# Batch 0's q and k by two hardware queues, its v ahead of w_in, and v's shifts by SyncE's queue

## The chip, the cores and the metric

The kernel runs on one core of one Trainium2 chip. The metric is the device time of one execution in microseconds. The engines are PE (matrix), PEld (its weight loads), DVE (vector), ACT (scalar), POOL (GpSimd) and SP (SyncE). Each runs its own instructions in the order in which the program was written, and waits on semaphores. SP and ACT issue DMAs on a hardware queue each, POOL issues DMAs on a software queue; a DMA that casts fp32 to bf16 on the way is issued by POOL here.

## The reference

```python
scores = q @ k.T / sqrt(64)                    # 8 batches, 8 heads, 576 positions, 64 wide
mask   = (0 <= i - j) & (i - j < 64)           # causal, a window of 64
attn   = softmax(where(mask, scores, -1e9))
x      = (attn @ v) -> 4608 tokens x 512       # heads side by side
h      = x @ w_in                              # 512 x 2048
out    = (h * sigmoid(h)) @ w_out              # 2048 x 512, fp32
```

All inputs are fp32 in DRAM.

## The kernel before, in words

**Attention.** Queries are cut into blocks of 64; a "visit" does 3 or 4 blocks of all 8 heads. Visits 0, 1, 2 are blocks 0 to 2, 3 to 5, 6 to 8: all of batch 0. A visit is a chain over four engines: scores on PE (`scores`, L298; for batch 0 the mask is first added by a matmul of `ident` with `bias`, L290), exp on ACT (L305), for later batches a mask product on DVE (L314), values on PE (`values`, L331), then on DVE the reciprocal (L337), the normalisation (L342) and a transpose into `bridge` (L350), which the feed-forward part reads. The scores of all visits use the PSUM banks 0 to 3, so a visit's scores wait for the exp of the visit before.

**Feed-forward.** Tokens go in tiles of 512 (j = 0 to 8; the first layer of j = 0 also does columns up to 576). The first layer is L360 (`first_layer`, `w_in_sb` in 16 column groups ft of 128, four matmuls each), silu on ACT is L366, the second layer is L369 for j = 0 and 1 and the products of L400 from j = 2 on. Exp and silu need different tables in ACT; a change of table is an ACT_TABLE_LOAD.

**Loads.** q and k of batches 0 and 1 come in three thirds c of 192 positions, for two groups Q of four heads: `load_rows` (L234) on POOL's queue, one DMA for each of q, k and Q. They land in `natq`, `natk`; DVE transposes them into `qt`, `kt` (L281). In batch 0's third 0, the heads of Q = 1 come as fp32 by `load_first` (L247), one DMA of 32 partitions for each head: q by SP's queue, k by ACT's; `cast_first` (L251) casts them. v comes in four groups g of 128 positions (`load_v`, L240) into `vo`, and 64 positions at the end straight into `ve` (L243). `ve` is v shifted by 64 positions, needed by even blocks; for batches 0 and 1 it is filled from `vo` by copies of half the partitions (`copy_v`, L262, DVE or ACT, up and down for each g), for later batches by two DMAs on SP's queue (L256, L258). w_in comes in 8 DMAs (L265), w_out in 8 (L269), by POOL's queue.

**What sets the order.** The kernel writes its operations down with costs, dependencies and ranks (`Plan.add`), and `Plan.run` simulates the engines and emits each engine's instructions in the order that its own model gives; operations of one class stay in the order in which they were added. So the order on POOL's queue is the order of the `p.add("dma", ...)` calls, and that on PE, ACT and DVE follows from the model's costs. When no attention work is ready, PE runs fillers on a tile of zeros (`warm`, L661) until the first layer has begun; their number and place are fixed by the plan. POOL's DMAs and the hardware DMAs each take eight semaphores in turn, so the ninth waits for the landing of the first.

In the kernel before, POOL issues: q and k of third 0 (Q = 0), v groups 0 and 1, w_in's first quarter (two DMAs), third 1, the constants `ident` and `window` (L191 to L199), v group 2, w_in's second quarter, third 2, v group 3 and the end of v, w_in's rest, w_out 0 to 3, then batch 1 with w_out 4 to 7 between its pieces. PE does the first layer of ft 0 to 3 for visit 0's columns (192 wide) between visits 0 and 1, the same for visit 1's columns before visit 2's values, and then ft 4 to 15 in widths of 384 and 192.

Of the kernel before, what the change touches and what calls it, by code (L numbers as in the profile page):

```python
# [15 lines left out]
class Plan:  # L16
# [10 lines left out]
        self.count = 0  # L27
        self.now = 0.0

    def add(self, cls, us, fn, deps=(), lat=0.1, gate=None, dma=None, pool=None, table=None, first=None):  # L30
        op = dict(us=us, first=self.rank[cls] if first is None else first, fn=fn, deps=[d for d in deps if d is not None],
                  lat=lat, gate=gate, dma=dma, pool=pool, table=table, seen=None, n=self.count, until=[], bank=None, cls=cls)
        self.count += 1
        self.queues.setdefault(cls, []).append(op)
        return op
# [13 lines left out]
    def run(self):  # L49
# [9 lines left out]
        while left:  # L59
            if not events:  # L60
                raise RuntimeError([(c, head[c], len(q), q[head[c]]["n"]) for c, q in self.queues.items() if head[c] < len(q)])
            now = self.now = heapq.heappop(events)
            while events and events[0] == now:
                heapq.heappop(events)
            moved = True
            while moved:
                moved = False
                for e in engines:
                    if free[e] > now:
                        continue  # L70
# [24 lines left out]
                    if op["table"] and op["table"] != table:  # L95
                        table, us = op["table"], us + 1.28
                    if e == "PE":
                        m = {"s": "rows", "v": "cols"}.get(c[0] if c in ("s", "v", "s0", "v0") else "", "full")
                        if m != mode:
                            mode, us = m, us + 0.1  # L100
                    end = free[e] = now + us
                    if op["dma"] is None:
                        op["seen"] = end + op["lat"]
                    else:
                        soft = e == "POOL"
                        begin = max(pipe[soft], end + (1.3 if soft else 0.8))
                        pipe[soft] = begin + op["dma"] * (1.0 if soft or pipe[True] < begin else 2.0)
                        op["seen"] = pipe[soft] + (2.2 if soft else 1.8) + (2.0 if soft and now > 45 else 0.0)
# [17 lines left out]
def kernel(ctx, tc, q, k, v, w_in, w_out, out):  # L126
    nc = tc.nc
# [45 lines left out]
    raw = gsum.rearrange("p s f t -> p (s f t)").bitcast(FP32)[:, 0:2 * NM * D].rearrange("p (k x) -> p k x", k=2)  # L173
# [5 lines left out]
    p = Plan(  # L179
        {"at": lambda: [(0, 1, 2, 3)], "two": lambda: [(4, 5), (6, 7)],  # L180
         "mp": lambda: [(i,) for i in (range(8) if att_end and p.done(att_end) else range(4, 8))]},
        rank=dict(one=-9, late=6, dma=-1, ldk=-9, ldq=-9, st=-2, vs=-3, silu=-3, out=-2, keep=-2.1, ssum=-1.2, tsum=1.2,
                  s=1, v=0, moe=99, warm=200, exp=1, mask=1, inverse=0, norm=0.1, cross=0.2, turn=2, cast=-4,
                  prime=-8, s0=-5.5, v0=-5.6, exp0=-4.6, inverse0=-4.3, norm0=-4.2, cross0=-4.25, turn0=-4, copy=1.5, copy0=-4.05),
    )
    copies = {"ACT": nc.scalar.copy, "DVE": nc.vector.tensor_copy, "POOL": nc.gpsimd.tensor_copy}

# [225 lines left out]

    rows_in, v_in, turned, turn_last = {}, {}, {}, {}
    s_last, v_last = {}, {}
    win, wout = {}, {}

# [33 lines left out]
    def add_first():  # L453
        for kk in range(2):
            rows_in[(0, kk, 0, 0)] = p.add("dma", {"POOL": 0.67}, lambda _, kk=kk: load_rows(0, kk, 0, 0), dma=0.55)
            ld = [p.add("ldk" if kk else "ldq", {"ACT" if kk else "SP": 0.45}, lambda _, kk=kk, h=h: load_first(kk, h), dma=0.14)
                  for h in range(4, 8)]
            rows_in[(0, kk, 0, 1)] = p.add("cast", {"ACT": 0.5, "DVE": 0.36}, lambda e, kk=kk: cast_first(e, kk), ld)

    def need_rows(vi):  # L460
        need = set()
# [5 lines left out]
    def need_v(vi):  # L467
        ops = []
        for x in range(vi["nb"]):
            b, t = divmod(vi["n0"] + x, NB)  # L470
            ops += v_in[(b, t // 2)] + (v_in[(b, t // 2 - 1)] if t % 2 == 0 and t else [])
        return list({o["n"]: o for o in ops}.values())


# [12 lines left out]
    def gate_scores(vi):  # L487
        def may():
# [3 lines left out]
            op, kind, rest, tile = x  # L492
            if tile < vi["tile"] - 2:
                return False
            if kind == 1:
                return not p.done(op["deps"]) and rest > 0
            return rest > 10
# [181 lines left out]
    c_ident = p.add("dma", {"POOL": 0.6}, const_ident)  # L679
    c_window = p.add("dma", {"POOL": 0.6}, const_window)  # L680
    c_bias = p.add("one", {"DVE": 0.5}, const_bias, [c_window])
    c_mask = p.add("late", {"DVE": 0.6}, const_mask, [c_window])
# [13 lines left out]
    add_w_out(5)  # L696
    add_rows(1, 1)
    add_v(1, 2)
    add_w_out(6)
    add_w_out(7)  # L700
    add_rows(1, 2)
    add_v(1, 3)
    add_v(1, 4)
    for c in range(NC):
        add_turns(0, c)
# [6 lines left out]
        add_turns(1, c)  # L712
    add_copies(1)
    gts = {0: {ft: (2 * ft, []) for ft in range(NFT)}, 1: {ft: (2 * ft + 1, []) for ft in range(NFT)}}
    for ft in range(0, 4):
        add_part(0, [ft], gts[0], 0, 192, 1)
    for ft in range(0, 4):
        add_part(0, [ft], gts[0], 192, 384, 1)
    for ft in range(4, 16):
        add_part(0, [ft], gts[0], 0, 384, 1)  # L720
    for ft in range(16):
        add_part(0, [ft], gts[0], 384, 576, 1)
        gts[1][ft][1].extend(gts[0][ft][1][-1:])
    add_second(0, gts[0], True)
    add_visit(visits[3])
# [71 lines left out]
```

## Time and profile before

| | |
|---|---|
| median of 3 runs | 334.33 us (299.22, 334.33, 415.25) |
| the profiled execution | 299.01 us |
| its span in the profile | 297.2 us |
| granted PE clock | 1.00 in every stretch |
| PE busy, with fillers | 281.5 us, 95% |
| DVE, ACT, POOL busy | 173.7, 166.0, 119.6 us |
| software DMA queue | 82656 packets, 18.20 MB |
| hardware queues of SP and ACT | 12.88 MB and 0.20 MB |

The profile is one execution. Its page gives the busy share by engine and slice, the chain of work that ended last and the costliest groups; beside it stand the timeline of each engine (start, duration, engine, line, tiles, count, and in brackets the idle time before and what ended it), sums over stretches, and the landings of DMAs. A DMA's landing is the last of the updates of its semaphore.

### The profile page before, as it was taken

How to read it: one execution, taken by the hardware profiler on the slowest of the kernel's cores; microseconds unless marked ns; L12 is line 12 of the kernel's file. 1: busy time of each engine (PE TensorE's matmuls, PEld its weight loads, DVE VectorE, ACT ScalarE, POOL GpSimd, SP SyncE). 2: the span in 40 equal slices, each digit the busy share in tenths (PEclk: the TensorE clock that was granted, in tenths of full speed). 3: DMA queues.
4: the chain of work that ended last, by engine and by line, in shares of the span. 5: the costliest groups of instructions: out<-in, count | busy, mean ns of one | idle time of the engine just before them, and what ended most of it. 6: DMA issues, size and time to landing. Idle time of an engine off the chain costs nothing.

```text
span 297.2 us, 9200 instructions
## 1 busy us (share of the span) xinstructions
PE 281.5 (95%) x4000; PEld 184.3 (62%) x4008; DVE 173.7 (58%) x327; ACT 166.0 (56%) x258; POOL 119.6 (40%) x183
## 2 busy tenths in 40 slices
PE   8973999999999999899999999999999999999993
PEld 4553584488444488447864686478647854884682
DVE  2464247561497498976986597469446944333412
ACT  1567792498618771767266835673477346316620
POOL 8787587887879779869600000000000000000000
PEclk9999999999999999999999999999999999999999
DMA  8999999999999999999996003000300030012003
GB/s 101 159 149 197 179 155 172 114 211 192 147 179 199 153 163 124 245 165 129 84 153 182 2 2 118 25 2 4 142 2 2 2 146 0 0 40 104 2 18 124
DMA packets 89512, 31.86 MB, mean 107 GB/s; under 512 B 76672, under 2 KB 84352, under 8 KB 89472
## 3 DMA queue, kind: packets, MB, share of 16 engines
q0 software_dynamic: 82656, 18.20, 66.4%
q1 hardware_dynamic: 6624, 12.88, 13.8%
q8 instruction: 31, 0.51, 0.7%
q10 hardware_dynamic: 192, 0.20, 0.2%
q14 instruction: 9, 0.07, 0.1%
HBM read 36.70 MB, written 9.44 MB: 155 GB/s over the span
## 4 chain that ended last, share of the span: by engine, by line
PE 76%; DMA 14%; POOL 5%; DVE 2%; issue 1%; DVEq 0%; POOLq 0%
PE ps L360 37%; PE ps L400 29%; DMA natq<-in_q_dram 8%; PE ps L369 5%; PE ps L331 3%; PE ps L298 3%; DMA w_in_sb<-in_moe_w_in_dram 3%; DMA ve<-in_v_dram 2%; POOL w_out_sb L269 1%; POOL vo L240 1%; DMA natk<-in_k_dram 1%; POOL natq L229 1%; POOL w_in_sb L265 1%; POOL natk L234 1%; POOL natq L234 1%
## 5 line engine op out<-in xcount | busy, mean ns | idle before, releaser
L360 PE MATMUL ps<-bridge,w_in_sb 128*128 128x512 bf16 (+3 forms) x720 | 127.4, 336 | 4.6 <-DVE bridge L350 2.8
L366 ACT ACTIVATE g<-ps 128x512 bf16<-128x512 f32 (+3 forms) x180 | 90.5, 512 | 43.3 <-PE ps L360 42.3
L360 PEld LDWEIGHTS <-w_in_sb 128*128 128x128 bf16 x720 | 67.8, 98 | 61.0 <-DVE bridge L350 3.0
L392 DVE TENSOR_TENSOR gsum<-g 128x512 bf16<-128x512 bf16 x56 | 23.5, 419 | 48.8 <-ACT g L366 48.8
L400 PEld LDWEIGHTS <-gsum 128*128 128x128 bf16 x448 | 43.2, 98 | 5.3
L400 PE MATMUL ps<-g,gsum 128*128 128x256 bf16 x336 | 42.6, 273 | 0.0
L305 ACT ACTIVATE e<-ps 128x2048 bf16<-128x2048 f32 (+1 forms) x19 | 34.0, 1787 | 13.8 <-PE ps L298 13.6
L400 PEld LDWEIGHTS <-g 128*128 128x128 bf16 x336 | 31.8, 98 | 4.6
L229 POOL DMA_DIRECT2D natk<-in_k_dram x48 | 28.9, 613 | 9.3 <-DMA vo<-in_v_dram 5.3
L240 POOL DMA_DIRECT2D vo<-in_v_dram x32 | 28.8, 915 | 6.5 <-PE ps L331 2.7
L229 POOL DMA_DIRECT2D natq<-in_q_dram x48 | 29.0, 620 | 3.3 <-issue 1.3
L403 ACT COPY part<-ps 128x256 f32<-128x256 f32 x27 | 10.1, 373 | 35.2 <-PE ps L400 35.2
L369 PE MATMUL ps<-w_out_sb,g 128*128 128x512 bf16 x120 | 27.6, 379 | 1.1 <-issue 1.0
L400 PE MATMUL ps<-w_out_sb,g 128*128 128x256 bf16 x224 | 26.8, 273 | 0.0
L314 DVE TENSOR_TENSOR e<-e,mask 128x2048 bf16<-128x2048 bf16 (+1 forms) x16 | 19.3, 1206 | 10.6 <-ACT e L305 10.3
L350 DVE STREAM_TRANSPOSE bridge<-ob 128x1024 bf16<-128x1024 bf16 (+1 forms) x19 | 22.3, 1173 | 0.2
L342 DVE TENSOR_TENSOR ob<-ps,rc 128x1024 bf16<-128x1024 f32 (+1 forms) x19 | 22.0, 1158 | 0.4
L412 DVE TENSOR_TENSOR ot<-ps,part 128x256 f32<-128x256 f32 (+1 forms) x35 | 16.2, 470 | 9.9 <-PE ps L400 5.4
L369 PEld LDWEIGHTS <-g 128*128 128x128 bf16 x128 | 11.8, 98 | 13.6
L281 DVE STREAM_TRANSPOSE qt<-natq 128x192 uint32<-128x192 uint32 x12 | 6.2, 519 | 19.4 <-DMA natq<-in_q_dram 19.4
L298 PEld LDWEIGHTS <-kt 32*128 32x128 bf16 x1152 | 10.7, 92 | 8.6 <-issue 5.9
L400 PE MATMUL ps<-g 128*128 128x256 bf16 x112 | 15.9, 273 | 0.0
(53 smaller groups left out, 226.3 us busy)
## 6 DMA issues: line engine op xcount, KB each, us to landing
out_dram<-ot SPq DMA_DIRECT2D x34, 256.0 KB, 3.0
vo<-in_v_dram POOLq DMA_DIRECT2D x32, 128.0 KB, 6.0
natq<-in_q_dram POOLq DMA_DIRECT2D x48, 72.0 KB, 5.1
natk<-in_k_dram POOLq DMA_DIRECT2D x48, 72.0 KB, 3.9
ve<-vo SPq DMA_DIRECT2D x12, 264.0 KB, 5.2
w_in_sb<-in_moe_w_in_dram POOLq DMA_DIRECT2D x8, 256.0 KB, 7.3
w_out_sb<-in_moe_w_out_dram POOLq DMA_DIRECT2D x8, 256.0 KB, 7.7
natq<-in_q_dram POOLq DMA_DIRECT2D x11, 96.0 KB, 7.7
```

Of the source, the lines that this page charges most:

```text
L229: nc.gpsimd.dma_start(out=nats[kk][b % NK][r, h // 4].rearrange("p c x -> p (c x)").rearrange("p (t x) -> p t x", x=2 * D), in_=(q, k)[kk] ...
L240: nc.gpsimd.dma_start(out=vos[b % NV][:, g, :, 0:D], in_=v[b, :, 128 * g:128 * g + 128].rearrange("h p d -> p h d"))
L298: nc.tensor.matmul(ps[:, j, 64 * s:64 * s + 64], lhsT=kts[b % NK][r, Q, 64 * t:64 * t + 128, h], rhs=qts[b % NK][r, Q, 64 * t:64 * t + 64, h],
L305: nc.scalar.activation(out=es[vi["i"] % NES][:, :, 0:ns].rearrange("p j s i -> p j (s i)"), in_=ps[:, 0:4, 0:64 * ns], func=ACTF.Exp, scal ...
L314: nc.vector.tensor_mul(e, e, m)
L342: nc.vector.tensor_mul(obs[vi["i"] % NOB][:, 0:4 * vi["nb"]].rearrange("p s (i x) -> p (s i) x", i=2).rearrange("p (b k) x -> p b k x", b= ...
L350: nc.vector.transpose(out=br.rearrange("p n Q u h i -> p (n Q u h) i"), in_=ob.rearrange("p s (h d) -> p (s h) d", h=2))
L360: nc.tensor.matmul(ps[:, bank["bank"][0], 0:hi - lo], lhsT=w_in_sb[:, c, ft * 128:(ft + 1) * 128], rhs=bridge[:, n0 + lo // 64:n0 + hi // ...
L366: nc.scalar.activation(out=g[:, lo:hi], in_=ps[:, bank["bank"][0], 0:hi - lo], func=ACTF.Silu)
L369: nc.tensor.matmul(ps[:, bank["bank"][0]], lhsT=gall[:, slot, m * 128:(m + 1) * 128], rhs=w_out_sb[:, f], start=(f == 0), stop=(f == NFT - 1))
L392: (nc.vector.tensor_sub if i else nc.vector.tensor_add)(out=t[i], in0=a, in1=b)
L400: nc.tensor.matmul(ps[:, bank["bank"][0], lo:lo + 256], lhsT=lhs, rhs=rhs, start=first, stop=last, skip_group_check=True)
```

## The change

- `load_first` now brings both head groups of a quarter of the partitions in one DMA (32 partitions x 2 x 384 fp32, 98 KB), and is used for thirds 0 and 1: eight DMAs on SP's queue for q, eight on ACT's for k. `cast_first` casts each (c, q or k, Q) on its own: eight casts, by ACT or DVE. Only third 2 is still loaded by POOL.
- POOL's order becomes: the constants, v groups 0 to 2, third 2, v group 3 and the end of v, all of w_in, w_out 0 to 3, and for batch 1 its third 2 and v group 3 ahead of w_out 6 and 7.
- ACT loads the exp table by a small activation between its two sets of q, k DMAs.
- For batch 0, v's group 0 and the upward half of group 1 are still copied; the other five halves, and all eight of batch 1, are DMAs of 64 partitions x 528 on SP's queue (`shift_group`). A visit waits only for the halves that it reads.
- The first layer of j = 0 is emitted for four ft at a time: 384 columns at once (visits 0 and 1 together), and the 192 of visit 2 behind the next four.
- The plan's model of DMA times, some ranks and the gate of the scores change. In the order that comes out, PE runs 46 fillers ahead of visit 0 (42 before), does all three visits of batch 0 before any first-layer matmul, and runs 27, 9 and 12 matmuls of L369 (10, 14 and 24 before) ahead of visit 5's values, between them and visit 6's, and behind visit 6's. On DVE two transposes of batch 3 stand within visit 6's chain. From the first layer of j = 2 on, PE's order is the same.

```diff
-    def load_first(kk, h):
-        r = slice(32 * (h % 4), 32 * (h % 4) + 32)
+    def load_first(c, kk, j):
         (nc.scalar if kk else nc.sync).dma_start(
-            out=raw[r, kk], in_=(q, k)[kk][0, h, 0:192].rearrange("(p m) d -> p (m d)", m=NM))
-    def cast_first(e, kk):
-        copies[e](out=nats[kk][0][:, 1, 0], in_=raw[:, kk])
+            out=raw[32 * j:32 * j + 32, c, kk],
+            in_=(q, k)[kk][0].rearrange("(Q j) s d -> j Q s d", j=4)[j, :, 192 * c:192 * c + 192].rearrange(
+                "Q (p m) d -> p Q (m d)", m=NM))
+    def cast_first(e, c, kk, Q):
+        copies[e](out=nats[kk][0][:, Q, c], in_=raw[:, c, kk, Q])
+    def shift_group(b, g, up):
+        vo, ve = vos[b % NV], ves[b % NV]
+        nc.sync.dma_start(out=(ve[64:128, g] if up else ve[0:64, g + 1]).rearrange("p h y -> p (h y)"),
+                          in_=(vo[0:64, g] if up else vo[64:128, g]).rearrange("p h y -> p (h y)"))
...
     def add_copies(b):
         for g in range(4):
-            v_in[(b, g)] = v_in[(b, g)] + [
-                p.add("copy" if b else "copy0", {"ACT": 0.66, "DVE": 0.35}, lambda e, up=up, g=g: copy_v(e, b, g, up), v_in[(b, g)]) for up in range(2)]
+            for up in (True, False):
+                if b == 0 and (g == 0 or (g == 1 and up)):
+                    op = p.add("copy0", {"ACT": 0.66, "DVE": 0.3}, lambda e, up=up, g=g: copy_v(e, b, g, up), v_in[(b, g)][0:1])
+                else:
+                    op = p.add("vs", {"SP": 0.45}, lambda _, up=up, g=g: shift_group(b, g, up), v_in[(b, g)][0:1], dma=0.2, slow=1.5)
+                v_sh[(b, g, up)] = op
...
-    add_first()
+    c_ident = p.add("dma", {"POOL": 0.6}, const_ident)
+    c_window = p.add("dma", {"POOL": 0.9}, const_window)
...
+    add_first(0)
+    p.add("ldk", {"ACT": 1.4}, lambda _: nc.scalar.activation(out=spare[:, 0:2], in_=spare[:, 2:4], func=ACTF.Exp), [c_spare])
+    add_first(1)
     add_v(0, 0)
     add_v(0, 1)
-    add_w_in(0)
-    add_rows(0, 1)
...
     add_v(0, 2)
-    add_w_in(1)
     add_rows(0, 2)
     add_v(0, 3)
     add_v(0, 4)
+    add_w_in(0)
+    add_w_in(1)
     add_w_in(2)
     add_w_in(3)
...
-    for ft in range(0, 4):
-        add_part(0, [ft], gts[0], 0, 192, 1)
-    for ft in range(0, 4):
-        add_part(0, [ft], gts[0], 192, 384, 1)
-    for ft in range(4, 16):
-        add_part(0, [ft], gts[0], 0, 384, 1)
-    for ft in range(16):
+    for f in range(0, NFT, 4):
+        for ft in range(f, f + 4):
+            add_part(0, [ft], gts[0], 0, 384, 1)
+        if f == 0:
+            continue
+        for ft in range(f - 4, f):
+            add_part(0, [ft], gts[0], 384, 576, 1)
+    for ft in range(NFT - 4, NFT):
         add_part(0, [ft], gts[0], 384, 576, 1)
```

More of the change, by code (lines that the diff above doesn't have):

```diff
@@ L105, in run @@
                         soft = e == "POOL"
-                        begin = max(pipe[soft], end + (1.3 if soft else 0.8))
+                        begin = max(pipe[soft], end + (2.0 if soft else 0.8))
                         pipe[soft] = begin + op["dma"] * (1.0 if soft or pipe[True] < begin else 2.0)
-                        op["seen"] = pipe[soft] + (2.2 if soft else 1.8) + (2.0 if soft and now > 45 else 0.0)
+                        op["seen"] = pipe[soft] + 1.8 + op["slow"] + (2.0 if soft and now > 45 else 0.0)
                         if soft:
@@ L181 @@
          "mp": lambda: [(i,) for i in (range(8) if att_end and p.done(att_end) else range(4, 8))]},
-        rank=dict(one=-9, late=6, dma=-1, ldk=-9, ldq=-9, st=-2, vs=-3, silu=-3, out=-2, keep=-2.1, ssum=-1.2, tsum=1.2,
+        rank=dict(one=-9, late=6, dma=-1, ldk=-9, ldq=-9, cast0=-5, cast1=-3.9, st=-2, vs=-3, silu=-3, out=-2, keep=-2.1, ssum=-1.2, tsum=1.2,
                   s=1, v=0, moe=99, warm=200, exp=1, mask=1, inverse=0, norm=0.1, cross=0.2, turn=2, cast=-4,
-                  prime=-8, s0=-5.5, v0=-5.6, exp0=-4.6, inverse0=-4.3, norm0=-4.2, cross0=-4.25, turn0=-4, copy=1.5, copy0=-4.05),
+                  prime=-9, s0=-5.5, v0=-5.6, exp0=-4.6, inverse0=-4.3, norm0=-4.2, cross0=-4.25, turn0=-4, copy=1.5, copy0=-4.05),
     )
@@ L449, in add_copies, with add_first @@
         for g in range(4):
-            v_in[(b, g)] = v_in[(b, g)] + [
-                p.add("copy" if b else "copy0", {"ACT": 0.66, "DVE": 0.35}, lambda e, up=up, g=g: copy_v(e, b, g, up), v_in[(b, g)]) for up in range(2)]
-    def add_first():
-        for kk in range(2):
[L455 to L458, printed above, removed]
+            for up in (True, False):
[4 more added lines that the diff above has]
+                v_sh[(b, g, up)] = op
+    def add_first(c):
+        for kk in range(2):
+            ld = [p.add("ldk" if kk else "ldq", {"ACT" if kk else "SP": 0.45}, lambda _, kk=kk, j=j: load_first(c, kk, j), dma=0.28)
+                  for j in range(4)]
+            for Q in range(2):
+                rows_in[(0, kk, c, Q)] = p.add(f"cast{c}", {"ACT": 0.5, "DVE": 0.36},
+                                               lambda e, kk=kk, Q=Q: cast_first(e, c, kk, Q), ld)
     def need_rows(vi):
@@ L470, in need_v @@
             b, t = divmod(vi["n0"] + x, NB)
-            ops += v_in[(b, t // 2)] + (v_in[(b, t // 2 - 1)] if t % 2 == 0 and t else [])
+            g = t // 2
+            if t % 2:
+                ops += v_in[(b, g)]
+            elif b < 2:
+                ops += ([v_sh[(b, g, True)]] if g < 4 else v_in[(b, g)]) + ([v_sh[(b, g - 1, False)]] if t else [])
+            else:
+                ops += v_in[(b, g)] + (v_in[(b, g - 1)] if t else [])
         return list({o["n"]: o for o in ops}.values())
@@ L494, in may @@
                 return False
+            if tile >= vi["tile"]:
+                return True
             if kind == 1:
@@ L672, in add_w_out @@
         wout[f] = p.add("dma", {"POOL": 0.68}, lambda _: load_w_out(f), dma=1.4)
-    add_first()
+    c_ident = p.add("dma", {"POOL": 0.6}, const_ident)
+    c_window = p.add("dma", {"POOL": 0.9}, const_window)
+    c_bias = p.add("one", {"DVE": 0.5}, const_bias, [c_window])
+    c_mask = p.add("late", {"DVE": 0.7}, const_mask, [c_window])
+    add_first(0)
+    p.add("ldk", {"ACT": 1.4}, lambda _: nc.scalar.activation(out=spare[:, 0:2], in_=spare[:, 2:4], func=ACTF.Exp), [c_spare])
+    add_first(1)
     add_v(0, 0)
     add_v(0, 1)
-    add_w_in(0)
-    add_rows(0, 1)
[L679 to L682, printed above, removed]
     add_v(0, 2)
-    add_w_in(1)
     add_rows(0, 2)
```

13 lines of the change are left out of this document (7 added, 6 removed).

## The prediction

> **What bounds the kernel now.** I read four views, in this order. First the sums over stretches (span of each, then PE, PEld, DVE, ACT, POOL busy, granted clock, DMA share, GB/s):
>
> ```profile
> 0.00:10.00 10.00, 9.01 (x38) 4.66 (x39) 4.34 (x20) 2.79 (x4) 8.63 (x18) 1.00 0.95 111
> 10.00:20.00 10.00, 8.87 (x192) 5.48 (x191) 4.63 (x11) 5.51 (x6) 8.15 (x13) 1.00 1.34 158
> 20.00:30.00 10.00, 4.65 (x168) 3.45 (x168) 5.13 (x10) 7.36 (x14) 7.10 (x11) 1.00 1.38 186
> 30.00:40.00 10.00, 10.00 (x79) 7.09 (x78) 3.95 (x9) 8.01 (x20) 6.70 (x10) 1.00 1.49 181
> ```
>
> From 30 us on PE is full and at clock 1.00; it stays so to the end but for about 2 us near 117 to 121. Only the first 30 us have something to give. PE's timeline says what is in them:
>
> ```profile
> 10.96 0.81 PE L290 MATMUL ps<-bias,ident 128*128 128x384 bf16 x4
> 12.19 1.47 PE L661 MATMUL ps<-idle 128*128 128x384 bf16 x8
> ...
> 14.38 1.15 PE L661 MATMUL ps<-idle 128*128 128x384 bf16 x6
> ...
> 23.62 0.48 PE L298 MATMUL ps<-qt,kt 32*128 32x64 bf16 x40 [1.49 <-DVE kt L281]
> 25.73 1.49 PE L360 MATMUL ps<-bridge,w_in_sb 128*128 128x192 bf16 x16 [1.62 <-DVE bridge L350]
> ```
>
> Fillers (L661) until 10.8, then the three visits of batch 0, spread over 18 us; dense first-layer work begins at 29.49 and ends at 42.66, where visit 3's scores begin. Visit 2's scores wait for third 2 of k: its last DMA landed at 23.02, v group 3 at 23.74, w_in's last quarter at 29.12. POOL's one queue feeds all of this. ACT's timeline adds three changes of table:
>
> ```profile
> 12.34 1.45 ACT L305 ACTIVATE e<-ps 128x1536 bf16<-128x1536 f32 x1 [2.07 <-PE ps L298]
> 18.91 1.28 ACT L366 ACT_TABLE_LOAD   x1
> 25.05 1.28 ACT L305 ACT_TABLE_LOAD   x1
> 26.35 1.45 ACT L305 ACTIVATE e<-ps 128x1536 bf16<-128x1536 f32 x1
> 27.81 1.28 ACT L366 ACT_TABLE_LOAD   x1
> ```
>
> Last, the DMA queues of 61 to 68 us, where SP's four stores meet POOL's v loads (packets, MB, share of 16 engines):
>
> ```profile
> q0 software_dynamic: 4317, 0.55, 122.1%
> q1 hardware_dynamic: 511, 0.92, 43.9%
> ```
>
> **The sum's base.** The profiled execution took 299.01 us, 1.81 around a span of 297.2. It is at the lowest of the three runs and 35 us under their median, 334.33; I forecast on its footing.
>
> **Part 1: when visit 0's exp starts.** It started at 12.34, and now waits for the latest of three things.
> (a) PE's order. 46 fillers stand ahead of the scores; the 42 of before ended at 10.77, the late ones 0.163 apart, so four more end at 11.42. The L290s and L298s took 1.38 from 10.96 to the exp: 12.80. The bias, which held L290 until 10.92, is no longer late: the constants took 1.42 on POOL (8.90 to 10.32) and now lead its queue.
> (b) The casts of third 1, which stand ahead of the exp on ACT. The queues must bring 16 x 98 = 1573 KB. From 2 to 4 us, nearly without POOL's traffic, 158 GB/s moved. POOL's first v DMA is issued at about 2.7 (1.25 plus the constants) and starts moving 2.4 later, as natq's did: 5.1. By then 490 KB are in. For the other 1083 KB I take the four stores: 1049 KB from 61.41 to 68.02, 159 GB/s beside POOL's v; so 11.9, and a cast of 0.51 gives 12.5. The low end is the two shifts L258 and L256, 528 KB in 69.65 to 75.46, 91 GB/s: 17.0. No gain is possible below (a).
> (c) On DVE the copy of v group 1 stands ahead of the last kt transpose. v's first group took 2.76 beside the stores (62.88 to 65.64), a third of its free pace of 0.85; v groups 0 and 1 so land at 7.9 and 10.6, and copy, transpose and scores (0.33, 0.5, 0.65 and 0.1) give 12.2.
> So the fillers decide: 12.80, with 0.3 us of cover over the queues.
>
> **Part 2: from that exp to dense work.** Nothing but the chain is left in it. The exp ends at 14.25; values 0.55 and L290 and L298 1.3, exp of visit 1 from 16.2 to 17.65; values 0.55, scores 1.25, exp of visit 2 from 19.55 to 21.0; values 0.6: dense work at 21.65. The fillers between (eight and six at 0.163) fit beside the exps. Three things must have come:
> - third 2, for the scores at 18.9: software work left at 11.9 is most of v group 2 (0.4), four row loads (0.75 each, from 34.3 to 37.5), so 15.3, plus four transposes at 0.38;
> - v group 3 (16.1) and its two shifts: two issues of 0.5 and a landing that took 1.9 to 4.75 for the 48 KB loads and 4.0 to 5.2 for the first shifts; with 3.5 it is 20.1, needed at 21.05. At 5.2 it costs 0.75;
> - w_in's first quarter: end of v 0.6, two DMAs at 1.3: 19.3. The next quarters come each 2.6 later, against needs 2.65 and more apart.
> The table load (1.28) runs from 21.0 beside the values and the first four ft.
> The first layer then has 64 matmuls of 384 and 64 of 192, 16 of 384 more than the 13.17 us of before from 29.49, at 0.65 per four: 2.6. It ends at 37.4 instead of 42.66: **minus 5.2**.
>
> The copies taken from ACT and DVE I cost at nothing: (a) and the chain hide them. If that cover went, three are 0.63 each on ACT.
>
> **Part 3: what waits behind.** Batch 1's loads follow on POOL. Before, 16.3 us passed from w_in's end to batch 1's v group 2; w_in now ends at 27.1, so third 0 lands at 35.5 (needed 37.4), third 1 at 42.6, third 2, now ahead of w_out 6 and 7, at 46 (visit 4's scores at 49.3), w_out 6 at 48.3 (needed 50.1), the shifts of group 3, which queue on SP in the order of v, at 52.8 (needed 53.9). All are covered, by 1 to 3 us; the eight copies that they replace lay off the path. Stores stand behind the shifts on SP, but their data come after 53.
>
> **Part 4: the order before tile 2.** 12 matmuls of L369 instead of 24 stand between visit 6's values and the first layer that needs visit 6. DVE's chain there now has the same five steps as visit 5's chain of before:
>
> ```profile
> 80.52 0.35 DVE L337 RECIPROCAL rc<-ps 128x32 f32<-128x32 f32 x1
> 80.79 0.72 DVE L279 STREAM_TRANSPOSE kt<-natk 128x576 uint32<-128x576 uint32 x1
> 81.43 1.18 DVE L342 TENSOR_TENSOR ob<-ps,rc 128x1024 bf16<-128x1024 f32 x1
> 82.54 0.75 DVE L279 STREAM_TRANSPOSE qt<-natq 128x576 uint32<-128x576 uint32 x1
> 83.22 1.20 DVE L350 STREAM_TRANSPOSE bridge<-ob 128x1024 bf16<-128x1024 bf16 x1
> ```
>
> 3.9 us from reciprocal to bridge, plus 0.2 from PE to DVE; PE's 12 matmuls last 2.5 (24 took 4.96), with 0.16 ahead. PE waits 1.5. Before it waited nothing. **Plus 1.6**, with the gap at the end. The weight sums behind (L385) come some 1.4 later against PE; DVE idled 1.6, 0.9, 1.9 and 1.7 us between 92 and 104, which takes that up. The end of the run has the same PE order as before, so the rest carries through.
>
> Sum: 299.0 - 5.2 + 1.6 = **295.4 us**, 1.2% less.
>
> [...]
>
> **Rivals.**
> 1. *The two queues crowd out v.* If POOL's queue moves nothing until q and k are in (12.0 at 158 GB/s), v group 1 lands at 13.7, DVE's queue stands at its copy, and visit 0's exp starts at 15.3: 2.5 later, **297.9**. For it: two queues instead of the stores' one. Against: in 4 to 6 us POOL's natq moved while hardware loads were still open.
> 2. *POOL's queue starves the two (the slower side).* The last fp32 loads of before, issued at 2.1, landed at 6.57 and 6.89, when POOL's packets had begun, and the first within 2.15. At the shifts' 91 GB/s third 1 lands at 17.0 and the exp starts at 17.6: 4.8 later, **300.2**. It turns the sign when the exp starts after 16.4, a rate under 101 GB/s. Against: the stores' 159.
> 3. *No wait before tile 2* (batch 3's transposes find a gap): minus 5.2 alone, **293.8**. Against: the order on DVE is fixed.
> 4. *The gain meets batch 1's loads.* If the stream after w_in slips 3 us (eight more hardware DMAs beside it), visit 4's values wait for their shifts some 2 us: **297.4**.
>
> **How the numbers follow.** Forecast 0.45, rivals 0.20, 0.15, 0.08, 0.12. The likeliest is 295.4; between the fillers' bound and rival 1 its own range is 294.5 to 297.9. The range over the cases is 293.8 to 300.2, which leaves out the deeper half of rival 2 and what is worked out nowhere here, under 0.2. A measurement of this kernel can tell about 2% from no change, 293.0 to 305.0. All cases lie within; faster needs 2.4 us more than the forecast has (0.08, no stall and a shorter chain together), slower needs q and k at under 60 GB/s (0.10); within 2%: 0.82.
>
> **What would show it.** Right: L298 of visit 0 ends near 12.7 straight behind the fillers, no ACT_TABLE_LOAD between the first three exps, the first layer's 384-wide matmuls from 21 to 22.5, visit 3's scores near 37.5, an idle of about 1.5 ahead of the first layer of tile 2. Wrong: ACT idle ahead of the first exp on gsum (rival 2), DVE idle on vo ahead of kt (rival 1), PE waiting for ve in visits 2 or 4 (rival 4).

## The result and the profile after

| | before | after |
|---|---|---|
| median of 9 runs | 300.08 us | 301.55 us |
| ratio, 95% interval | 1 | 1.0062 [1.0044, 1.008] |
| the profiled execution, its span | 299.01, 297.2 us | 301.66, 299.9 us |
| first exp starts | 12.34 | 15.50 |
| first layer of tile 0, its dense part | 29.49 to 42.66 | 26.93 to 45.38 |
| first layer of tile 2 starts | 89.27 | 92.74 |

The forecast was 295.4 us, 1.2% less; measured is 0.6% more, and above the range. (Three of the runs of before, 303.6, 334 and 415 us, lie over 1.5% above its fastest and are left out of the ratio.) In the two profiled executions the loss is all there at 45 us (2.7 us behind), grows to 3.5 at tile 2, and ends at 2.7; over the runs of the ratio it is 1.9.

The sums over stretches of the changed kernel (span, then PE, PEld, DVE, ACT, POOL busy, granted clock, DMA share, GB/s):

```profile
0.00:10.00 10.00, 9.01 (x44) 4.90 (x45) 4.11 (x22) 2.92 (x5) 8.40 (x18) 1.00 1.30 159
10.00:20.00 10.00, 6.27 (x170) 3.51 (x168) 6.79 (x16) 3.98 (x6) 5.85 (x9) 1.00 1.58 193
20.00:30.00 10.00, 5.74 (x158) 3.31 (x159) 4.84 (x7) 3.88 (x5) 5.34 (x8) 0.78 1.23 209
30.00:40.00 10.00, 10.00 (x71) 6.70 (x70) 1.92 (x4) 6.85 (x18) 7.13 (x10) 0.88 1.52 179
```

Two things differ from before. PE is busy 6.27 us of the second stretch, where it was 8.87. And the granted clock, the share of its full clock that PE was given, is 0.78 and 0.88, where every row of before has 1.00: the trace's record of it is 0.50 from 25.55 to 32.37, and 1.00 otherwise but for the last 1.3 us. PE is "10.00 busy" from 30 to 40, but with 71 matmuls where before had 79.

ACT's timeline says why the second stretch is empty:

```profile
12.62 0.92 ACT L252 CAST natq<-gsum 128x384 bf16<-128x384 f32 x2 [2.50 <-DMA gsum<-in_q_dram]
15.08 0.51 ACT L252 CAST natk<-gsum 128x384 bf16<-128x384 f32 x1 [1.54 <-DMA gsum<-in_k_dram]
15.50 1.44 ACT L311 ACTIVATE e<-ps 128x1536 bf16<-128x1536 f32 x1
```

The scores of visit 0 were done at 12.2. The exp came 3.3 later, since third 1's casts stand ahead of it on ACT and their data were late (the waits for `gsum` above): the eight loads of third 0 had landed by 7.55, the last of third 1 at 14.98, 786 KB in 7.43 us, 106 GB/s. That is rival 2's mechanism.

PE's timeline carries the other two losses:

```profile
17.00 0.32 PE L337 MATMUL ps<-ve,e 128*32 128x66 bf16 x16 [3.33 <-ACT e L311]
...
23.86 0.32 PE L337 MATMUL ps<-ve,e 128*32 128x66 bf16 x16 [1.58 <-ACT e L311]
24.00 0.32 PE L337 MATMUL ps<-vo,e 128*32 128x66 bf16 x16
24.15 0.24 PE L337 MATMUL ps<-ve,e 128*32 128x66 bf16 x6
26.65 0.35 PE L337 MATMUL ps<-ve,e 128*32 128x66 bf16 x10 [2.26 <-issue]
26.93 18.51 PE L366 MATMUL ps<-bridge,w_in_sb 128*128 128x384 bf16 x128
```

In the middle of 16 equal matmuls, with all operands there, PE stands still for 2.26 us, and no semaphore ends it ("issue"). Then the first layer takes 18.45 us for work that I had put at 15.77, at half clock for its first 5.4 us.

Before tile 2 the forecast wait is there, 1.38 us for 1.5:

```profile
88.82 2.54 PE L375 MATMUL ps<-w_out_sb,g 128*128 128x512 bf16 x11 [0.16 <-issue]
92.74 3.61 PE L366 MATMUL ps<-bridge,w_in_sb 128*128 128x512 bf16 x16 [1.38 <-DVE bridge L356]
```

So three suspects: the hardware queues' rate beside POOL's loads; a stop of PE with no visible cause; a halved clock.

### The profile page after: what moved, and what is told of

Same layout as the page of the kernel before. It is cut to its first block, busy times and chain, and to the rows that moved or that the text cites. A ratio compares the mean times of both kernels' runs of the same rounds, so it can differ in the third digit from the quotient of the medians.

```text
span 299.9 us, 9190 instructions
## 1 busy us (share of the span) xinstructions
PE 282.4 (94%) x3985; PEld 183.7 (61%) x3992; DVE 171.0 (57%) x322; ACT 161.5 (54%) x251; POOL 114.9 (38%) x177
## 4 chain that ended last, share of the span: by engine, by line
PE 76%; DMA 13%; POOL 3%; issue 3%; ACT 2%; DVE 1%; ACTq 1%; POOLq 0%
PE ps L366 38%; PE ps L406 25%; PE ps L375 6%; DMA vo<-in_v_dram 5%; DMA gsum<-in_k_dram 4%; PE ps L337 3%; DMA natk<-in_k_dram 3%; PE ps L304 3%; ACT e L311 1%; POOL natk L229 1%; DMA natq<-in_q_dram 1%; POOL natq L229 1%; POOL vo L240 1%; ACTq L246 1%; PE ps L296 1%
## 5 line engine op out<-in xcount | busy, mean ns | idle before, releaser
L366 PE MATMUL ps<-bridge,w_in_sb 128*128 128x512 bf16 (+3 forms) x704 | 129.3, 345 | 2.6 <-DVE bridge L356 2.5
L311 ACT ACTIVATE e<-ps 128x2048 bf16<-128x2048 f32 (+1 forms) x19 | 34.0, 1787 | 22.4 <-PE ps L304 22.3
L375 PE MATMUL ps<-w_out_sb,g 128*128 128x512 bf16 x121 | 27.8, 379 | 0.8 <-issue 0.6
L418 DVE TENSOR_TENSOR ot<-ps,part 128x256 f32<-128x256 f32 (+1 forms) x35 | 16.2, 469 | 9.5 <-PE ps L406 5.0
L375 PEld LDWEIGHTS <-g 128*128 128x128 bf16 x128 | 12.0, 98 | 13.8
L337 PEld LDWEIGHTS <-e 128*32 128x32 bf16 x1152 | 11.4, 98 | 13.4 <-ACT e L311 6.3
L337 PE MATMUL ps<-ve,e 128*32 128x66 bf16 x640 | 11.7, 200 | 7.2 <-ACT e L311 4.9
```

The lines of the kernel that those rows point to most:

```text
L311: nc.scalar.activation(out=es[vi["i"] % NES][:, :, 0:ns].rearrange("p j s i -> p j (s i)"), in_=ps[:, 0:4, 0:64 * ns], func=ACTF.Exp, scal ...
L337: nc.tensor.matmul(pv[32 * j:32 * j + 32, sub // k, sub % k], lhsT=e[:, j, s, 32 * u:32 * u + 32], rhs=w[:, 4 * Q + j].rearrange("p (x i) ...
L366: nc.tensor.matmul(ps[:, bank["bank"][0], 0:hi - lo], lhsT=w_in_sb[:, c, ft * 128:(ft + 1) * 128], rhs=bridge[:, n0 + lo // 64:n0 + hi // ...
L375: nc.tensor.matmul(ps[:, bank["bank"][0]], lhsT=gall[:, slot, m * 128:(m + 1) * 128], rhs=w_out_sb[:, f], start=(f == 0), stop=(f == NFT - 1))
```

## The experiments

Ratios are to the kernel before, from runs on the same chip, with 95% intervals; the changed kernel's is 1.0062 [1.0044, 1.008].

**1. Fillers in the waits** (the changed kernel; in `values`):

```diff
+        for _ in range({0: 18, 1: 3, 2: 9}.get(vi["i"], 0)):
+            nc.tensor.matmul(ps[:, op["bank"][0], 0:384], lhsT=idle, ...)
```

> The changed kernel with 30 more fillers on PE: 18 ahead of visit 0's values, 3 ahead of visit 1's, 9 ahead of visit 2's, where PE stood idle for 3.3, 0.5 and 1.6 us. Theory A (the dense first layer took 18.45 us instead of 15.8 because the idle PE had lost its clock: 0.50 granted from 25.55 to 32.37): the clock stays at 1.00 through 20 to 40 us, the stretch takes about 15.8, and the run about 298.9, 2.7 under the changed kernel. Rival (the clock fell for another reason, or PE was held by silu or w_in): still 0.50 near 26 to 32, about 301.5. Theory B for the 2.3 us in the middle of visit 2's third group of values, which no semaphore explains (PE had run out of instructions, 705 matmuls and loads in): the gap comes at the same place in PE's stream, so about 30 matmuls earlier in visit 2's values, and is there or shorter. Rival (a late transfer): the gap stays in the third group.

Measured: 298.08 us, ratio 0.9929 [0.9902, 0.9957]. More work on PE made the kernel faster. The two views, stretches and PE's timeline:

```profile
20.00:30.00 10.00, 8.42 (x186) 5.31 (x186) 4.49 (x6) 5.55 (x8) 4.89 (x7) 1.00 1.23 210
30.00:40.00 10.00, 10.00 (x88) 7.61 (x87) 1.96 (x4) 8.08 (x22) 7.02 (x10) 1.00 1.70 168
```

```profile
23.43 1.62 PE L332 MATMUL ps<-idle 128*128 128x384 bf16 x9 [1.58 <-ACT e L311]
24.98 0.32 PE L340 MATMUL ps<-ve,e 128*32 128x66 bf16 x16
...
25.52 15.85 PE L369 MATMUL ps<-bridge,w_in_sb 128*128 128x384 bf16 x128
```

The clock stays at 1.00, and the first layer takes 15.79 us, the 15.77 of the prediction; so the halved clock cost 2.7. The mean clock was 0.999 or 1.000 in all four runs; in the nine of the changed kernel it was 0.974 to 0.989. The nine fillers of visit 2 did not fill its wait: they waited for the exp too, and held the values for 1.6. Yet the stop of 2.26 us in the third group is gone, where theory B had it earlier and at most shorter. Dense work starts at 25.52.

**2. POOL's v loads held back** (the changed kernel; four memsets on POOL ahead of the first v load, which is then issued at 9.57 instead of 2.08):

```diff
     add_first(1)
+    for _ in range(4):
+        p.add("dma", {"POOL": 0.01}, lambda _: nc.gpsimd.memset(oall, 0.0))
     add_v(0, 0)
```

> The changed kernel with four memsets of the output tile on POOL ahead of its first v load, so that POOL's queue starts some 5 us later or more and the fp32 loads run alone for longer. Theory (v's loads took the hardware queues' share: third 1 landed at 14.98, 110 GB/s after 5.1): alone they go on at about 158 GB/s, third 0 lands near 7 (7.55) and third 1's last k by 12 to 12.5. Rival (the two queues are slow by themselves, by their issue and eight semaphores in flight): third 1 still lands at 14.5 to 15. The run's time as a whole says little, since v and third 2 come later: 301 to 306.

Measured: 303.83 us, a single run. Third 1 landed at 9.42 instead of 14.98. Counted from 2 us on, thirds 0 and 1 (1573 KB) came at 212 GB/s, and in the changed kernel at 121. So it was POOL's traffic beside them that made the two hardware queues slow, not the queues, nor the shape of their transfers. The loss only changed places: v came at 13.2 to 15.8, DVE stood at its copy of v ahead of kt (rival 1's mechanism), and visit 2 waited 2.44 us for a shift.

**3. w_in behind batch 0, and nothing else** (the kernel before):

```diff
-    add_w_in(0)
...
-    add_w_in(1)
...
+    add_w_in(0)
+    add_w_in(1)
     add_w_in(2)
```

> The kernel before with one part of the change alone: w_in's first two quarters go behind batch 0's q, k and v on POOL's queue; q and k of thirds 1 and 2 stay with POOL. Theory (POOL's queue is a stream, and what stood ahead of third 2 was w_in; the hardware queues brought third 1 only 0.7 us earlier than POOL had): third 2 lands about 5 us earlier than at 23.0, w_in's first quarter near 21, dense work starts near 24, and the run takes 297 to 298.5, under both kernels. Rival (the fp32 loads are what a reorder needs, or PE's clock falls here too): 300 or more.

Measured: 296.58 us, ratio 0.9877 [0.985, 0.9905], faster than both kernels. (The plan's order on PE follows the edit: 36 fillers ahead of visit 0 for 42, and 16 first-layer matmuls stand around visit 2's scores, 2 ahead and 14 behind.) By POOL's queue alone third 1 landed at 10.6 to 12.2, before the two hardware queues' 14.98, and the first exp starts at 11.71. The clock is 1.00 to the end. PE's timeline again shows stops with no semaphore, one in visit 1, one in visit 2:

```profile
16.87 0.20 PE L331 MATMUL ps<-ve,e 128*32 128x66 bf16 x1
18.57 0.32 PE L331 MATMUL ps<-ve,e 128*32 128x66 bf16 x15 [1.50 <-issue]
...
25.04 0.27 PE L331 MATMUL ps<-vo,e 128*32 128x66 bf16 x9 [1.02 <-issue]
```

**4. Batch 3's two transposes behind visit 6's chain on DVE** (the changed kernel; a reordering of what the plan emitted):

```diff
+        part = order[at["inverse"]:at["cross"] + 1]
+        late = [x for x in part if x[0]["cls"] == "turn"]
+        order[at["inverse"]:at["cross"] + 1] = [x for x in part if x[0]["cls"] != "turn"] + late
```

> The changed kernel with batch 3's two transposes moved out of visit 6's chain on DVE to behind its last step; nothing else is moved. Theory (PE's 1.38 us ahead of tile 2's first layer is that chain): the wait falls to 0.4 or less and the run takes 300.4 to 300.6. Rival (something else is late next, such as the banks or the table load): 301.5.

Measured: 300.17 us, ratio 0.999 [0.9955, 1.0024]. The wait ahead of tile 2 fell from 1.38 to 0.38:

```profile
92.51 13.97 PE L370 MATMUL ps<-bridge,w_in_sb 128*128 128x512 bf16 x64 [0.38 <-DVE bridge L360]
```

So Part 4's term is what it was said to be, and avoidable.

**5. Third 1 by POOL again** (the changed kernel; only third 0 by the hardware queues):

```diff
-    add_first(1)
     add_v(0, 0)
+    add_rows(0, 1)
     add_v(0, 1)
```

> The changed kernel, but third 1 of batch 0's q and k is loaded by POOL's casting DMAs again (right behind v group 0); only third 0 stays with the two hardware queues. Theory (hardware queues beside POOL's v loads got 110 to 115 GB/s, so third 1 came at 14.98 us): third 1 lands by 9 to 12 us, as in e3_winlate (10.62 to 12.15), no casts of it stand on ACT, visit 0's exp starts at 12.3 to 13 instead of 15.50, visit 1's scores no longer wait for kt, dense work starts at 21.5 to 24; 294.5 to 298 us, the upper end if PE's idle time halves the clock. Rival (the memory traffic as a whole is the limit, whichever queue carries it): third 1 lands at 14 to 15 here as well, the exp of visit 1 stays at 18 to 19, 300.5 to 302 us.

Measured: 303.74 us, ratio 1.0105 [1.0069, 1.0142]: the time missed, the mechanism held. Third 1 landed at 9.2 to 10.8, and the three exps start at 12.35, 15.78 and 19.36, where the prediction had 12.80, 16.2 and 19.55. Why dense work started at 25.30 all the same is on PE's timeline:

```profile
18.02 0.23 PE L304 MATMUL ps<-qt,kt 32*128 32x64 bf16 x7
18.79 0.49 PE L304 MATMUL ps<-qt,kt 32*128 32x64 bf16 x41 [0.54 <-issue]
...
22.31 0.33 PE L337 MATMUL ps<-ve,e 128*32 128x66 bf16 x16 [2.49 <-DMA ve<-vo]
...
23.07 0.25 PE L337 MATMUL ps<-ve,e 128*32 128x66 bf16 x7 [0.28 <-DMA ve<-vo]
25.02 0.35 PE L337 MATMUL ps<-ve,e 128*32 128x66 bf16 x9 [1.71 <-issue]
```

Once third 1 is on time, the shifts of v group 3 are late: issued at 17.26 and 17.77, landed at 22.18 and 23.02. PE stops at 25.02 again, and the clock is 0.50 from 23.51 to 30.33. Later the plan came out with 2 matmuls of L375 (L369 of before) instead of 12 behind visit 6's values, so PE waited 3.96 ahead of tile 2 and the clock halved there too (91.77 to 98.60).

**6. Batch 0's v halves all by copies** (the changed kernel):

```diff
-                if b == 0 and (g == 0 or (g == 1 and up)):
+                if b == 0:
```

> The changed kernel, but all eight halves of batch 0's v are copied by ACT and DVE again; batch 1's stay with SP's queue. Theory (the shifts of batch 0 were covered: visit 2's values waited for exp, not for ve): no more than 0.7 us to either side of the changed kernel's 301.5, with the wait ahead of visit 2's values still ended by exp, and the clock still halved for one stretch. Rival (the shifts' 5 to 6 us of latency, or their traffic, delayed visit 2 and so brought the idle time): dense work starts 1 us or more sooner and the clock stays up; 297 to 299 us.

Measured: 299.68 us, ratio 0.9961 [0.9928, 0.9995], which neither side had. Visit 2's values wait for exp here as well (0.23), and the stop of PE is there (1.42). In the profiled run the clock was halved from 16.28 to 23.11, so during the sparse chain and not in the first layer. The eight of its runs that are in the ratio spread from 298.1 to 301.2 (two more took 302.6 and 303.0), those of the changed kernel from 301.1 to 302.4. Whether the copies won this 1% or the place of the half clock did stays open.

**7. Fillers ahead of visits 0 and 1 alone** (`{0: 18, 1: 3}` in the diff of 1):

> The changed kernel with 18 fillers ahead of visit 0's values and 3 ahead of visit 1's, and none ahead of visit 2's (e1_fill had 9 there, which held the values by 1.6 us). Theory of the clock (the idle 3.3 us ahead of visit 0's values starts what halves it): clock 1.00 through the first layer, which then takes 15.8 us. Theory of the instruction supply (PE ran dry at a fixed place of its stream, since the next 16 KB came late): 21 more matmuls stand ahead, so the place falls some 40 instructions sooner, in the first or second group of visit 2's values or within the wait for exp; dense work starts at 24 to 25.5. Together 296.5 to 298 us. Rival (the idle time just ahead of the dense work alone drops the clock): 0.50 for some 6.8 us again and 299.5 to 301 us.

Measured: 299.25 us, ratio 0.9963 [0.9933, 0.9993]. Dense work starts at 25.41. The stop fell in the second group of visit 2's values, as expected of 21 more matmuls, behind 2 of its 16; the changed kernel's was behind 6 of the third group, 20 matmuls later. The clock did halve, from 24.67 to 28.08, one stretch of 3.41 instead of two. So filling the first two waits is not enough. Nor did experiment 1's last nine fillers cost the 1.6 that they held the values for: with them dense work started at 25.52, without them at 25.41.

**8. Experiments 4, 5 and 6 together:**

> Three edits together: third 1 by POOL (as e5), batch 0's v halves all by copies (as e6), batch 3's two transposes behind visit 6's chain on DVE (as e4). If the parts add: the gain of e5 and some 1.0 from the wait ahead of tile 2 (1.38 to 0.4): 293 to 297 us, faster than e3_winlate's 296.6 if the clock stays up. Rival (waits of PE that were filled by data now lie bare, and the clock halves): 298 to 300 us.

Measured: 297.65 us, ratio 0.9921 [0.9882, 0.996]. Faster than before, not faster than experiment 3, and between the two ranges. Exps at 12.41, 15.84 and 19.82; again two stops, then half clock from 23.62 to 27.03:

```profile
17.98 0.23 PE L341 MATMUL ps<-vo,e 128*32 128x66 bf16 x5 [0.35 <-issue]
...
23.90 0.36 PE L341 MATMUL ps<-ve,e 128*32 128x66 bf16 x12 [1.92 <-issue]
```

Here the places of the stops can be counted. Each matmul of bf16 is two of PE's instructions, a weight load and the product (the changed kernel's page has 3992 of PEld and 3985 of PE). From the program's order, the instructions ahead of each stop of over 0.19 us in the first 30 us:

| kernel | first stop behind | us | second stop behind | us |
|---|---|---|---|---|
| after | - | - | 700 | 2.26 |
| 3 | 446 | 1.50 | 702 | 1.02 |
| 4 | - | - | 700 | 1.10 |
| 5 | 446 | 0.54 | 702 | 1.71 |
| 6 | - | - | 702 | 1.42 |
| 7 | 446 | 0.20 | 702 | 0.54 |
| 8 | 446 | 0.35 | 702 | 1.92 |

The work at these places differs (scores, first, second or third group of values); the number is 446 for the first and 700 or 702 for the second, 256 apart. The trace has a DMA queue for this, which the page of the changed kernel lists:

```profile
q8 instruction: 31, 0.51, 0.8%
```

That is 31 packets of 16 KB for some 7990 instructions of PE, so about 256 in each. After each of these stops PE goes on 2.2 to 3.2 us after such a packet began to move. I read this as PE having run out of instructions; experiments 10 to 12 move the count and test it. Before came to its 702nd only at 27.9, and has no such stop in the first 30 us.

**9. Experiment 5 with the reordering of 4:**

> e5_pool1 (third 1 by POOL) with batch 3's two transposes moved behind visit 6's chain on DVE, as in e4_turns. In e5 the planner's order changed ahead of tile 2 as well: 2 matmuls of L369's kind stood behind visit 6's values, PE waited 3.96 us for bridge and the granted clock was 0.50 for the 6.83 us after it. Theory (e5 lost by that alone what third 1's earlier landing had won): the wait ahead of tile 2 falls to 1 us or less (two transposes of 0.8 less, and 0.4 where 1.38 was), the clock stays up there, and the time falls by 4 to 6 us against e5's 303.7, to 297.5 to 299.5. Rival (the cost of e5 lies in the first 45 us): 302 to 304 us again.

Measured: 303.22 us, ratio 1.0112 [1.0077, 1.0147]. A miss. The wait ahead of tile 2 stayed at 3.97: in this plan it isn't transposes that stand between visit 6's steps on DVE but weight sums (L395, 0.63 to 0.68 each), which my edit didn't move, and the clock fell there again (93.68 to 97.10). And visit 2 waited 5.16 us for the shifts. It does show once more that the shifts bind when q and k are early.

**10. Experiment 8 with 3 fp32 fillers for 18 of bf16.** Each is longer and takes fewer instructions; in the trace an fp32 matmul is two matmuls of 0.39 us (one filler takes 0.91, two take 1.56, where eight of bf16 took 1.47 in the kernel before).

```diff
+        if warmed[0] > 45:
+            if warmed[0] % 4 == 1:
+                nc.tensor.matmul(ps[:, op["bank"][0], 0:384], lhsT=idle32, ...)
+            return
```

> e8_best1, but the 18 fillers of the plan that stand behind visit 0's scores are replaced by three of fp32, each one instruction pair that lasts about four times as long (0.65 us). In e4 to e8 PE stood still with no semaphore behind its 700th to 702nd instruction, in e3, e5, e7 and e8 also behind its 446th, 256 before. Theory (a 16 KB piece of PE's own instructions, 256 of them, comes too late): the places stay at 446 and 702 in the stream, so they move 12 and 15 matmuls later in the work: behind 7 matmuls of the second group of visit 1's values, and behind 3 or so dense matmuls after visit 2's values; PE goes on some 6 us after it passed the 446th, so dense work is not held as long: its first layer ends 0.5 to 1.5 us earlier than 40.87; 296 to 297.3 us. Rival (the idle time is tied to visit 2's third group, by its banks or its operands): the gap stays in that group.

Measured: 297.16 us, ratio 0.9897 [0.9864, 0.993], no different from experiment 8. The stop moved with the count, counted as the trace counts fp32: behind 13 of the third group, 702 again:

```profile
21.51 0.31 PE L344 MATMUL ps<-ve,e 128*32 128x66 bf16 x13
24.48 0.24 PE L344 MATMUL ps<-ve,e 128*32 128x66 bf16 x3 [2.66 <-issue]
```

PE went on at 24.48, hardly other than 23.90: fewer instructions ahead of the stop made it later in the work, not shorter in time. The first layer ended at 42.02, not before 40.87, with the clock at 0.50 from 22.07 to 28.90; so the time lies in the forecast's range without the forecast's reason.

**11. The same fillers in experiment 3** (24 become six):

> e3_winlate (the kernel before, with w_in's first half behind batch 0's q, k and v) with the 24 fillers behind visit 0's scores replaced by six of fp32. By the instruction theory the places of 446 and 702 move 13 and 18 matmuls later in the work: to the end of the second group of visit 1's values, and from behind 7 matmuls of visit 2's second group to behind 9 of its third. The gaps shrink from 1.50 and 1.02 us to about 1.3 and 0.8, so 295.8 to 296.6 us, unclear against e3's 296.58. Rival (long fillers in front of a visit's work hold it up to 0.65 us each): 297 to 298 us.

Measured: 297.71 us, ratio 0.9921 [0.9898, 0.9945]. The first stop is behind 9 of the second group, 446 with fp32 counted twice (0.85 us for 1.50); the second is gone. Dense work starts at 25.38 as in experiment 3, now after a wait of 1.03 for silu. Nothing won. The time is the rival's, but the first layer ends at 39.87, as in experiment 3 (39.89), so what the 1.1 us more are stays open.

**12. More instructions early** (experiment 3; 14 fillers ahead of visit 0 split in halves, six later ones doubled):

```diff
+        for x in [192, 192] if 6 < k <= 20 else [384, 384] if k > 54 else [384]:
+            nc.tensor.matmul(ps[:, op["bank"][0], 0:x], lhsT=idle, ...)
```

> e3_winlate with two edits to the fillers alone: 14 of the 36 ahead of visit 0's scores are split in two of half the width (the same PE time, 28 instructions more), and the six ahead of the first two matmuls of L360 become twelve. Theory (PE's instructions come in pieces of 256; the next piece is called for when a boundary is passed, comes 5.5 to 6.5 us later, and the boundaries lie at 190, 446 and 702): more instructions early make the first boundary pass 1.5 us sooner (in visit 0's scores at 11.5 instead of 13.0), so the piece behind 446 comes by about 17.0 instead of 18.57, where PE gets to it then (behind 3 matmuls of visit 1's first group of values): a gap of 0 to 0.5 us instead of 1.50. The piece behind 702 comes by 23.5 instead of 25.04; 702 then lies in visit 2's first group: a gap under 0.3 instead of 1.02. Dense work starts at 24.2 to 24.8 instead of 25.39; 295.3 to 296.2 us. Rival (the gaps belong to the values' work, or more instructions only mean more to fetch): gaps of 1.5 and 1.0 us in the second groups again, and with 1 us of fillers added 296.6 to 297.6 us.

Measured: 296.02 us, ratio 0.9867 [0.9833, 0.9901]; not to be told from experiment 3.

```profile
16.57 0.21 PE L332 MATMUL ps<-vo,e 128*32 128x66 bf16 x3
18.32 0.30 PE L332 MATMUL ps<-vo,e 128*32 128x66 bf16 x13 [1.54 <-issue]
...
25.49 14.56 PE L361 MATMUL ps<-bridge,w_in_sb 128*128 128x192 bf16 x128 [1.03 <-ACT g L367]
```

The place came out to the matmul: behind 3 of the first group, 446. The time didn't: the stop is 1.54 and not under 0.5, and dense work starts at 25.49 and not by 24.8, so that 296.02 lies in the range is luck. PE passed its 190th instruction at 11.24 (in experiment 3 at 12.54), the packet of the next piece began at 15.13 (15.71), and PE went on at 18.32 (18.57). Passing the boundary 1.3 us sooner won 0.25. The second stop is gone.

The other traces still fit the assumption that a piece is called for when PE passes the boundary 256 instructions ahead of it. The first packet began 2.2 to 4.2 us after PE had passed its 190th in all fourteen kernels: at 14.1 to 16.2 where it passed it at 11.2 to 13.0, and at 19.79 in experiment 2, where the late v held PE until 16.30. The second began 2.4 to 4.7 us after PE had passed its 446th, between 17.6 and 23.8. At the fourteen stops PE went on 5.2 to 7.1 us after it had passed the boundary before. So in these traces 256 instructions in less time than that ended in a stop; why the wait varies, and was 7.1 here, stays open.

## Why the prediction was wrong, point by point

- **What bounds it, and the base.** Right: all the difference but 0.8 us at tile 2 arose in the first 45 us. The base of 299.0 was that of one execution; the median of before came out at 300.08. That execution was a lucky one in its clock as well: in the 62 runs of before that stand beside the experiments the mean clock is 0.979 to 1.000, on average 0.991, and only 7 have 0.999 or more. So stretches at half clock are not new in the changed kernel (0.985 on average), and some of the 2.7 us that they cost it against the profile of before are lost in most runs of before too; how much is not known.
- **Part 1, (a) and (c).** The fillers' bound was right: experiment 5, without the wait for third 1, has its first exp at 12.35 for 12.80. The constants did come off the path (the bias at 2.43).
- **Part 1, (b): failed.** "For the other 1083 KB I take the four stores ... 159 GB/s". Third 1 came at 106 GB/s (110 by the prediction's count, 1083 KB from 5.1 on), so the exp at 15.50: 2.7 late. The row was misread: 61.41 is when the first store began to land, but the stores' packets began at 60.28, so the 1049 KB took 7.74 us, 136 GB/s, which by the same sum gives 13.6 and no cover at all. And it was the wrong row: it has one hardware queue that writes, where here two read; the end that I gave as the low one, 91 GB/s, was nearer. Experiment 2 shows the two queues fast without POOL's loads (212 GB/s from 2 us on, for 121 in the changed kernel), so the loss comes from the meeting of the three. I had this as rival 2, with the turn of the sign under 101 GB/s, and gave it 0.15. At 110 it alone would have left a small gain. Rival 1 did not happen: v groups 0 to 2 landed at 8.04, 10.06 and 11.91, between the landings of the hardware loads (third 0's last at 7.55, third 1's at 14.98). So no queue was shut out; how the three shared out the bytes no run here shows.
- **Part 2, "Nothing but the chain is left in it": failed.** The steps of the chain were right (experiment 5: exps 3.4 and 3.6 apart for 3.4 and 3.35). But two supplies were not on my list. The first is PE's own instructions: a stop of 2.26 us here, of 0.2 to 2.7 elsewhere. In twelve kernels with chains of quite different waits, dense work starts at 24.2 at the earliest, never at the 21.65 that I gave. My estimate from the table and the figures of experiment 12: the 190th instruction lies in visit 0's scores, at about 12, and the 702nd at the end of visit 2, two pieces or 10.4 to 14.2 us later, so with these counts dense work would hardly start before 22.4. The second is the shifts of v group 3, which I had landing at 20.1, with "at 5.2 it costs 0.75". In experiment 5 they landed at 22.18 and 23.02 and cost 2.8; in the changed kernel the late exps hid them.
- **Part 2, "dense work" at full clock: failed, and in no rival.** 0.50 for 6.83 us, 2.7 us by experiment 1. Before, PE's waits in the chain were many and up to 1.62; the change has 3.33 in one piece, and 1.58 with 2.26 close behind it, and it was within the latter that the clock fell.
- These three, 2.7 + 2.6 + 2.7, are the 8.0 us by which the first layer ended later than forecast (45.38 for 37.4); of the 2.6, 2.26 are PE's stop. They do not add from kernel to kernel: with third 1 on time (experiment 8) PE stops for 0.35 and 1.92, and dense work starts at 24.19, 2.7 sooner than here and still 2.5 later than forecast. Tile 2 began 7.1 later than forecast, and the span ended 6.3 later; the later tiles gave back the rest.
- **"The copies taken from ACT and DVE I cost at nothing".** Not settled (experiment 6).
- **Part 3.** Right: PE waits for none of batch 1's loads or shifts.
- **Part 4.** Right: 1.38 for 1.5, and experiment 4 takes it away.
- **The sign.** Of the change's parts, moving w_in behind batch 0's loads alone gains 1.2% (experiment 3). The rest takes away more than that.

## What to carry to other kernels

A transfer moved to another queue is not a transfer on its own (the same 1573 KB came at 212 GB/s alone and at 121 beside POOL's loads): price it by a row in which as many queues of that kind, in that direction, meet, and let the far end carry the forecast if no row does. When a stretch is made denser, count what it uses up besides engines and data: here PE's instructions, 256 to a piece, of which some 200 go into one short visit (the stop behind the 700th took 2.26 us). And waits that lie close together can cost in clock as well, 2.7 us here for 1.58 and 2.26, so a plan's fillers belong into the waits that come out, not into those of its model. Last, one profile is one draw of the clock (means of 0.979 to 1.000 in 62 runs of before): look at the clock of several runs before its time becomes the base of a sum.

## What the runs showed of the hardware that I had not expected

- **The clock.** Before the kernel's end, stretches at 0.50 last 3.41 or 6.83 us in all nine kernels that have one. In two kernels the drops lie a whole number of such steps apart: those of the changed kernel, at 25.55 and near its end at 298.61, 273.07 us or 80 of 3.413; those of experiment 5, at 23.51 and 91.77, 68.26 us or 20. If time is cut into windows of 3.41 from a drop back, PE's idle time in the window ahead of a drop was 1.61, 1.78 and eleven times 1.94 to 3.17 us; windows that kept the clock had up to 1.86. So in these traces some half of such a window was enough, and 1.6 to 1.9 went either way. The window ahead of the changed kernel's drop at 25.55 held 1.58 us of one wait and 1.16 of the next. The wait of 3.33 us dropped nothing there: two windows share it and hold 1.64 and 1.69 us of idle time. In experiments 4 and 6 a like wait (3.29 and 3.47) put 2.59 and 2.31 into one window, and the clock fell. The windows lie differently in each run (counted from the span's start, the grid of experiment 7's drop at 24.67 begins at 0.78, that of experiment 8's at 23.62 at 3.14). So by my estimate what a wait costs differs too, which fits the spread of experiments 4 and 6 (3.3 and 3.1 us from lowest to highest).
- **PE's instructions.** They come in pieces of 16 KB on a queue of their own (31 packets in the changed kernel), and PE stood still behind its 446th and 702nd, 256 apart, for 0.2 to 2.66 us. From 30 us on, where the dense matmuls last 0.11 to 0.22 us, little of this is left: four of the kernels, before among them (0.40), have one stop of 0.29 to 0.44 us between 139 and 150 us, 2.2 to 2.4 us after a packet began. The stops came where 100 matmuls, visit 1's values and the bias and scores of visit 2, take 1.85 us; there the next piece came 5.2 to 7.1 us after PE had passed the boundary before it.
- **The queues.** 212 GB/s for two hardware queues alone, 121 for the same loads beside POOL's casting loads of v and third 2; meanwhile POOL's third 1 in experiments 3 and 5 came sooner than the hardware queues' did.
